# Another order of the first pair's copies, bits, maxima, scores and values, and of ScalarE's work in the last pairs, in a bucket-masked attention with a rational FFN

## The chip, the core and the metric

The kernel runs on one core of one Trainium2 chip. The metric is the device time of one execution in microseconds. Engines are named as the profile names them: PE (TensorE, with PEld for its weight loads), DVE (VectorE), ACT (ScalarE), POOL (GpSimd) and SP (SyncE, whose queue issues most DMAs).

## The reference

For 4 batches x 8 heads, 768 tokens and 64 channels, each query and key gets a 6-bit bucket from the signs of a projection. Scores between different buckets are masked; softmax and the product with V follow. The result is laid out as 3072 tokens x 512 channels and goes through an FFN whose nonlinearity is a rational function.

```python
q_bits = (np.einsum('bhsd,dk->bhsk', q, proj) > 0)      # likewise k_bits
mask = q_bucket[:, :, :, None] == k_bucket[:, :, None, :]
scores = np.where(mask, scale * q @ k.T, -1e9)
scores = scores - scores.max(-1)
attn = np.exp(scores); attn = attn / (attn.sum(-1) + 1e-9)
out = attn @ v
h = x @ w_in                                             # 512 -> 2048
g = (a0 + a1*h + a2*h**2 + a3*h**3) / (1 + |b0|*|h| + |b1|*h**2 + 1e-6)
y = g @ w_out                                            # 2048 -> 512
```

## The kernel before

**Pairs and steps.** The 32 heads are taken in 16 pairs (two heads of one batch). A pair has twelve steps: step s covers half `s // 6` of the queries (384 columns) and key tile `s % 6` (128 keys). `scores(p, s)` computes, for both heads, two accumulating matmuls of 128x384 into a PSUM bank of tag "s" (three banks, name `pss`), and ACT takes the exponential into one of seven E tiles; POOL adds E tiles into sums. `values(p, s)` multiplies V with the E tile of a step into the single bank of tag "v" (name `psv`); `values_out` copies the finished half out on ACT (a 1-column copy `col`, then `xo`). Each `scores` step is four matmul instructions in the profile, each `values` step four as well (plain float32, issued as two passes), and a `maxstep` two.

**Maxima ahead of the scores.** Before a pair's scores, its row maxima are found: `maxstep(p, j)` is one pass over all 768 keys for 128 queries of one head (bank pair of tag "psa", two of them, name `psm`) and a DVE reduction of 128x768. `shift_turn`, or `first_shift` for pair 0, turns the maxima into a row of the query operand (name `pst`), so that the score matmul subtracts them. The mask is done by extra rows of the operands as well: `bits`, `first_bits` and `second_bits` project queries and keys (name `psb`), DVE compares with zero, `penalties` scales on ACT, and `maskrows` moves the rows by DMA.

**Copies.** Queries and keys are split into a rounded part (`high`, an ACT cast of 128x768) and a remainder (`low`). For pair 0 the second head's operands are placed by extra ACT copies of 64x768, `first_cross`, in place of DMAs. `first_penalties` writes mask rows of pair 0's queries.

**The order is written out by hand.** Every piece of work is put in the dictionary `plan` by `at(p, s, function, ...)` at place 12 p + s; the places are decimals from the tables `MID` (pairs 1 to 14), `FIRST` (pair 0) and `LAST` (the last pairs). The plan is walked in order of place, and each engine, and SP's DMA queue, executes its instructions in just that order: an instruction that waits holds all that stands behind it on its engine. `warm(n)` issues n matmuls on a tile of zeros whose result nothing reads. `weights(i)` brings the FFN weights (stored as float64) in between: a DMA `wr`, ACT conversions `ws` and `wr`, DVE steps and a final ACT cast.

**FFN.** From the last pair on, `Ffn.step` runs GEMM 1 (`psh`), the rational terms, and GEMM 2 (`pso`) in blocks of 512 tokens.

Nearly all instructions are recorded by one helper line, 94 in the kernel before and 96 in the changed one; so they are told apart here by tile names.

Of the kernel before, what the change touches and what calls it, by code (L numbers as in the profile page):

```python
# [7 lines left out]
F32 = mybir.dt.float32  # L8
# [5 lines left out]
ALU = mybir.AluOpType  # L14
# [4 lines left out]
P = 128  # L19
S = 768  # L20
HQ = 384
NT = S // P
# [3 lines left out]
NPAIR = B * NHP  # L26
# [5 lines left out]
NFC = DFF // P  # L32
# [17 lines left out]
FIRST = dict(  # L50
    maxima1=[-0.04, -0.02, 5.52, 5.97, 6.42, 6.87, 7.32, 7.77, 8.22, 8.67, 9.12, 9.57], maxima2=9.5, rate2=0.82, high=[3.25, 3.53],
    low=[6.0, 7.3], bits=7.15, penalties=7.25, high_move=4.53, maskrows=8.2, second_low=-26.5, second_high=4.35, load_v=4.78, group=2,
    values=[-1.07, 2.65, 2.32, 2.35, 0.35, 0.61], values_out=3.02, high1=[-3.0, -3.2], low1=[-2.8, -2.95],
    high_move1=-2.7, load2=-2.6, load3=3.8, load4=9.0, penalties1=-24.26, maskrows1=-24.2,
    weights=[[-27.25, 6.64, 6.7, 11.42, 12.19, 18.75, 23.03], [8.03, 9.04, 9.24, 11.12, 14.81, 15.27, 15.99, 17.91, 46.81]],
    warm0=9, warm1=1, warm=3, warms=[3, 3, 3, 1, 1, 1], maxima00=[-4.3, -2.3, -4.2, -0.9, -1.2, -0.8], shift00=[-1.0, -0.2],
    shift0=[-0.08, -0.06], ahead=3, scores=[[-0.5, -0.4, -0.1], [0.1, 0.3, 0.4]], pen01=[-2.9, -0.35],
    second_high0=[-3.42, -3.4, -3.3, -3.25], load_v0=-3.3, bits1=-0.3, comp1=[-0.28, -0.27],
    maxima0=[-24.05, -23.8, -23.5, -0.9, -0.7, -0.1], turn1=[8.46, 13.26], rows1=[9.59, 14.35], turn2=8.61, third=6.9,
    third_weights=[1.44, 5.1, 5.5, 8.5, 9.5, 11.02, 11.035], steps={3: -1.0, 4: -0.8, 5: -0.6, 6: 5.4, 7: 6.5},  # L60
)
# [112 lines left out]
def attention(ctx, tc, nc, raw, ps_b, tail, tokens, early, operands_to_terms, ffn, load, QF, KF, v, w_in, w_out, wo_d, ident, cst, ones, prj,  # L174
# [147 lines left out]
    def first_cross(t):  # L322
        F, T = ((QF, Q1), (KF, K1))[t]
        nc.scalar.copy(T[0][0:64, 1 - t, :], F[0][64:128])
# [16 lines left out]
                                scalar1=-CLAMP, scalar2=-1.0, op0=ALU.max, op1=ALU.mult)  # L341


    def second_bits():
        for hf in range(2):
            ps = AV[1, hf] = ps_b.tile([P, 512], F32, tag="vs"[hf], bufs=(1, 3)[hf], name=f"psb1_{hf}")
            for t, F in enumerate((QF[1], KF[1])):
                o = 64 + 32 * t
                nc.tensor.matmul(ps[o : o + 32, 0:HQ], prj[:, t, :], F[:, hf * HQ : hf * HQ + HQ], start=True, stop=True)

    def second_compare(hf):
        nc.vector.tensor_scalar(out=MB[1][0][64:128, hf, :], in0=AV.pop((1, hf))[64:128, 0:HQ], scalar1=0.0,
                                scalar2=cst[64:128, 0:1], op0=ALU.is_gt, op1=ALU.subtract)

    def scores(p, s, heads=(0, 1)):
        hf, kt = divmod(s, NT)
# [119 lines left out]
    def at(p, s, f, *args):  # L476
        plan.setdefault(12 * p + s, []).append((f, args))
# [4 lines left out]

    for p in range(NPAIR):
        mid = 0 < p < NPAIR - 1
        n = MID["group"] if mid else (FIRST if p == 0 else LAST)["group"]
        for s in range(12):
            if p > 0 or s >= FIRST["ahead"]:
                at(p, FIRST["steps"].get(s, s) if p == 0 else s, scores, p, s)

            if p > 1:  # L490
                at(p - 2, FIRST["maxima2"] + FIRST["rate2"] * s if p == 2 else FIRST["third"] if p == 3 and s == 0 else MID["maxima"][s], maxstep, p, s)
            if s % n == n - 1:
                for i in range(s - n + 1, s + 1):
                    at(p, s + (MID["values"][s // n] if mid else (FIRST if p == 0 else LAST)["values"][s // n]), values, p, i)
            if s % NT == NT - 1:
                at(p, s + (LAST["vout14"] if (p, s) == (NPAIR - 2, 11) else MID["values_out"][s // n] if mid else (FIRST if p == 0 else LAST)["values_out"]), values_out, p, s // NT)
        for hf in range(2):
            at(p, 6 * hf + 9, values_store, p, hf)
        if p < NPAIR - 1:
            at(p, MID["sums"] if p < NPAIR - 2 else LAST["sums14"], sums, p)  # L500
            at(p, MID["sums_store"] if p < NPAIR - 2 else LAST["sumst14"], sums_store, p)
        if p > 1:
            for t in range(2):
                at(p - 2, (MID if p > 2 else FIRST)["high"][t], high, p, t)
                at(p - 2, MID["low"][t + t * p % 2] if p > 2 else FIRST["low"][t], low, p, t, nc.vector if p > 2 else nc.gpsimd)
# [12 lines left out]
        if p > 3:
            at(p - 4, MID["load"] if p > 4 else FIRST["load4"], load, p)
        if p % NHP == NHP - 1 and p + 1 < NPAIR:  # L520
            spread(p, MID["recips"], recips(p // NHP))
    for i in range(2 * NFC):
        o = 12 * (i // 2)
        w = list(FIRST["weights"][i]) if i < 2 else list(MID["weights"][i % 2])
        if i == 2:
            w = list(FIRST["third_weights"])
        if i == 2 * NFC - 4:
            w[0] = LAST["weights14"]
        if i == 2 * NFC - 1:
            w = w[:-4] + [w[-5] + x for x in MID["weights_last"]]  # L530
        spread(0, [o + x for x in w], weights(i))
# [29 lines left out]
    for h in range(2):  # L561
        for i in range(3):
            at(-2, FIRST["maxima00"][3 * h + i], maxstep, 0, NT * h + i)
            at(-2, FIRST["maxima00"][3 * h + i] + 0.01, warm, FIRST["warms"][3 * h + i])
# [268 lines left out]
```

## Time and profile before

| | us |
|---|---|
| median of three timed runs | 928.65 |
| the three runs | 1526.64, 928.65, 927.13 |
| profiled execution, device time | 924.78 |
| its span | 923.0 |
| PE busy | 914.9 (99%) |
| DVE busy | 839.9 (91%) |
| ACT busy | 653.7 (71%) |
| POOL busy | 425.7 (46%) |

The span is the time from the first to the last record of the profiled execution; 1.78 us lie around it. PE works without a visible break from about 8.4 us to the end, so that what counts of any other engine is the time for which PE has to wait for it. Busy shares over the whole span say little on the two stretches that the change touches: the first 50 us (pair 0 and the run into pair 1) and the stretch from 361 to 395 us (pairs 14 and 15, before the FFN). The granted clock of TensorE reads 1.00 in every stretch.

### The profile page before, as it was taken

To read this page: it belongs to the slowest core of one execution; us is meant where nothing else is said; L and a number is where in the kernel's file an instruction comes from. 1 tells how busy PE (TensorE), PEld (TensorE's weight loads), DVE (VectorE), ACT (ScalarE), POOL (GpSimd) and SP (SyncE) were. 2 spreads that over 40 slices of the span, in tenths; PEclk is the share of its full clock that TensorE was granted. 3 is DMA by queue.
4 is the path that set the end of the run, shared out by engine and by line. 5 is a ranking of instruction groups with operands and counts; after the bars stand their busy time and mean duration, and the time that the engine had idled before them with its cause. 6 is when DMAs were issued, how large, how long until landed. Compare 5 with 4: busy or idle time off the path is not lost.

```text
span 923.0 us, 13657 instructions
## 1 busy us (share of the span) xinstructions
PE 914.9 (99%) x4673; PEld 699.3 (76%) x4673; DVE 839.9 (91%) x1021; ACT 653.7 (71%) x1227; POOL 425.7 (46%) x363
## 2 busy tenths in 40 slices
PE   8999999999999999999999999999999999999998
PEld 5567767676767676678888888888888888888886
DVE  6799989988989899688998999999999989998996
ACT  7467777777777777886777677767676777667664
POOL 6577777677777777612322222222223222322221
PEclk9999999999999999999999999999999999999999
DMA  7678878787878778444402100400040013001001
GB/s 238 178 206 224 239 204 249 212 234 216 239 207 238 199 211 240 151 191 165 141 1 95 43 1 1 137 1 0 1 137 1 1 39 99 1 1 46 1 0 46
DMA packets 51097, 111.57 MB, mean 121 GB/s; under 512 B 9330, under 2 KB 19942, under 8 KB 51028
## 3 DMA queue, kind: packets, MB, share of 16 engines
q1 hardware_dynamic: 50596, 110.34, 40.4%
q8 instruction: 37, 0.61, 0.3%
q10 hardware_dynamic: 432, 0.36, 0.1%
q14 instruction: 32, 0.26, 0.1%
HBM read 56.82 MB, written 21.17 MB: 84 GB/s over the span
## 4 chain that ended last, share of the span: by engine, by line
PE 97%; DVE 1%; ACT 0%; DMA 0%; issue 0%; POOL 0%; POOLq 0%; ACTq 0%
PE psh L94 28%; PE pso L94 28%; PE pss L94 15%; PE psv L94 14%; PE psm L94 7%; PE psu L94 2%; PE psb L94 1%; DVE m L94 1%; DMA qkf<-qT 0%; PE pst L94 0%; PE pst_None L94 0%; POOL lo L94 0%; DVE ws L94 0%; ACT q L94 0%; ACT E L94 0%
## 5 line engine op out<-in xcount | busy, mean ns | idle before, releaser
L94 POOL TENSOR_TENSOR gl<-c,gh 128x512 fp32r<-128x512 f32 x95 | 135.8, 1429 | 384.7 <-ACT gh L94 374.6
L94 PE MATMUL pso<-wo,gh 128*128 128x512 f32 x768 | 235.9, 389 | 0.0
L94 DVE TENSOR_REDUCE m<-psm 128x1 f32<-128x768 f32 x192 | 180.6, 953 | 28.6 <-PE psm L94 21.0
L94 ACT ACTIVATE E<-pss 128x384 f32<-128x384 f32 x384 | 166.8, 492 | 40.2 <-PE pss L94 32.3
L94 POOL TENSOR_TENSOR acc<-E,E 128x384 f32<-128x384 f32 x124 | 146.2, 1198 | 95.7 <-ACT E L94 95.7
L94 PE MATMUL pss<-q,k 128*128 128x384 f32 (+2 forms) x768 | 171.2, 346 | 0.9 <-ACT E L94 0.7
L94 PEld LDWEIGHTS pso<-wo,gh 128*128 128x128 f32 x768 | 144.2, 188 | 29.9
L94 ACT ACTIVATE h<-psh 128x512 f32<-128x512 f32 x96 | 57.4, 598 | 132.9 <-PE psh L94 132.8
L94 PEld LDWEIGHTS pss<-q,k 128*128 128x128 f32 (+2 forms) x768 | 134.5, 190 | 22.1 <-issue 8.0
L94 PE MATMUL psh<-xh,wi_hi 128*128 128x512 f32 x384 | 149.6, 390 | 0.0
L94 PE MATMUL psh<-xl,wi_hi 128*128 128x512 f32 x384 | 149.4, 389 | 0.0
L94 PE MATMUL psh<-xh,wi_lo 128*128 128x512 f32 x384 | 149.4, 389 | 0.0
L94 PE MATMUL pso<-wo,gl 128*128 128x512 f32 x384 | 148.9, 389 | 0.0
L94 DVE SCALAR_TENSOR_TENSOR c<-c,ab,r 128x512 f32<-128x512 f32 x96 | 138.7, 1445 | 0.0
L94 POOL TENSOR_TENSOR acc<-acc,E 128x384 f32<-128x384 f32 x123 | 132.5, 1096 | 3.4 <-ACT E L94 3.0
L94 PE MATMUL psv<-E,v 128*64 128x385 f32 x768 | 131.9, 492 | 0.0
L94 PE MATMUL psm<-k,q 76*128 76x384 f32 (+1 forms) x384 | 100.6, 344 | 1.8 <-ACT k L94 1.5
L94 PEld LDWEIGHTS psv<-E,v 128*64 128x64 f32 x768 | 52.0, 137 | 65.5 <-issue 63.6
L94 DVE SCALAR_TENSOR_TENSOR w<-h,absb,w 128x512 f32<-128x512 f32 x96 | 72.9, 759 | 15.2 <-ACT w L94 15.0
L94 PEld LDWEIGHTS psh<-xh,wi_hi 128*128 128x128 f32 x384 | 72.0, 188 | 16.0 <-issue 1.2
L94 PEld LDWEIGHTS psh<-xh,wi_lo 128*128 128x128 f32 x384 | 72.1, 188 | 15.0
L94 PEld LDWEIGHTS pso<-wo,gl 128*128 128x128 f32 x384 | 72.0, 188 | 15.0
(77 smaller groups left out, 1213.1 us busy)
## 6 DMA issues: line engine op xcount, KB each, us to landing
q<-q SPq DMA_DIRECT2D x45, 192.0 KB
k<-k SPq DMA_DIRECT2D x45, 192.0 KB
wr<-w_in SPq DMA_DIRECT2D x16, 512.0 KB
wr<-w_out SPq DMA_DIRECT2D x16, 512.0 KB
wo_d<-wr SPq DMA_DIRECT2D x16, 512.0 KB
wo<-wo_d SPq DMA_DIRECT2D x16, 512.0 KB
qkf<-qT SPq DMA_DIRECT2D x16, 384.0 KB
qkf<-kT SPq DMA_DIRECT2D x16, 384.0 KB
```

What stands on the lines that cost most here:

```text
L94: return self.tc.keep_in_program_order(issue(*args, **kwargs))
```

## The change

Four things are edited, most of them by numbers in the tables.

- `first_cross(1)`, the copy of k for the first head, is issued ahead of `high(0, 1)` in place of behind the comparisons.
- `second_bits`, the projection for pair 1's bits, is split in its two halves, both in one bank of tag "v", and the halves go between the first maxima of pair 0. Eight of the twelve warm matmuls that stood between maxima go.
- In pairs 0 and 1 the maxima, scores and values take new places: the values of pair 0 are issued one step at a time, in place of in groups of two and more, between single maxima and scores. The bits and mask rows of pair 2, the shift rows of pair 1, and the loads of V for pair 1 and of one `w_out` block take new places with them.
- In pairs 14 and 15 some ACT work takes new places: `values_out` of pair 14's first half and of pair 15, and the conversions of three weight blocks.

```diff
 FIRST = dict(
...
-    values=[-1.07, 2.65, 2.32, 2.35, 0.35, 0.61], values_out=3.02, high1=[-3.0, -3.2], low1=[-2.8, -2.95],
+    values=[-0.4, -0.07, -0.03, 5.0, 5.2, 5.3, 6.3, 7.4, 8.2, 9.1, 9.6, 10.4], values_out=[5.31, 10.42], high1=[-3.0, -3.2],
...
 LAST = dict(
-    group=6, values=[0.28, 0.44], values_out=1.39, vout14=3.03,
+    group=6, values=[0.28, 0.44], values_out=0.46, vout14=[3.5, 3.03],
+    hi14=17.05, weights15=[5.1, 5.11],
...
-    def second_bits():
-        for hf in range(2):
-            ps = AV[1, hf] = ps_b.tile([P, 512], F32, tag="vs"[hf], bufs=(1, 3)[hf], name=f"psb1_{hf}")
-            for t, F in enumerate((QF[1], KF[1])):
-                o = 64 + 32 * t
-                nc.tensor.matmul(ps[o : o + 32, 0:HQ], prj[:, t, :], F[:, hf * HQ : hf * HQ + HQ], start=True, stop=True)
+    def second_bits(hf):
+        if hf == 0:
+            MS[2] = ps_b.tile([P, 512], F32, tag="v", name="psb1")
+        for t, F in enumerate((QF[1], KF[1])):
+            o = 64 * hf + 32 * t
+            nc.tensor.matmul(MS[2][o : o + 32, 0:HQ], prj[:, t, :], F[:, hf * HQ : hf * HQ + HQ], start=True, stop=True)
...
-            if s % n == n - 1:
+            if p == 0:
+                at(p, FIRST["values"][s], values, p, s)
+            elif s % n == n - 1:
...
     warm(FIRST["warm1"])
+    first_cross(1)
     high(0, 1)
...
     first_compare(0, 1)
-    first_cross(1)
     low(0, 1, nc.gpsimd)
...
-    at(-2, FIRST["bits1"], second_bits)
     for hf in range(2):
+        at(-2, FIRST["bits1"][hf], second_bits, hf)
         at(-2, FIRST["comp1"][hf], second_compare, hf)
```

**PE, the first maxima of pair 0.** The names are `psm0_j` for the maximum step j of pair 0, `psw` for a warm matmul, `pst0_0_0` for the turn of the first three maxima, `psb1` for pair 1's bits and `pss0_s_h` for a score step of head h. Before:

```order
L94 MATMUL psm0_1_260<-k1_0_177,q1_0_179 128x384 x2
L94 LDWEIGHTS E6_153
L94 MATMUL psw5_264<-E6_153 128x384
L94 LDWEIGHTS E6_153
L94 MATMUL psw5_264<-E6_153 128x384
L94 LDWEIGHTS E6_153
L94 MATMUL psw5_264<-E6_153 128x384
L94 MATMUL psm0_7_268<-k1_0_177,q1_0_179 128x384 x2
L94 LDWEIGHTS E6_153
L94 MATMUL psw6_272<-E6_153 128x384
L94 MATMUL pst0_0_0_274<-cst_75,m0_214 1x128 x3
L94 MATMUL psm0_6_279<-k1_0_177,q1_0_179 128x384 x2
```

After, from the second maximum on:

```order
L96 MATMUL psm0_2_223<-k1_0_177,q1_0_179 128x384 x2
L96 MATMUL psb1_227<-qkf1_77,prj_73 32x384 x2
L96 MATMUL psm0_1_259<-k1_0_177,q1_0_179 128x384 x2
L96 MATMUL psb1_227<-qkf1_77,prj_73 32x384 x2
L96 MATMUL psm0_7_265<-k1_0_177,q1_0_179 128x384 x2
L96 LDWEIGHTS E6_153
L96 MATMUL psw4_269<-E6_153 128x384
L96 MATMUL pst0_0_0_271<-cst_75,m0_214 1x128 x3
L96 MATMUL psm0_6_276<-k1_0_177,q1_0_179 128x384 x2
L96 MATMUL pss0_0_0_280<-q1_0_179,k1_0_177 128x384
L96 MATMUL pss0_0_0_280<-q2_0_202,k2_0_203 128x384
L96 MATMUL psm0_8_284<-k1_0_177,q1_0_179 128x384 x2
```

In place of the warm matmuls stand the two halves of pair 1's bits, two matmuls each, and the first scores now stand between `psm0_6` and `psm0_8`. In the kernel before the four bits matmuls stood in one piece behind `pss0_1_0`.

**ACT, from the end of pair 0's scores to the start of pair 1's.** The names are the E tiles, `ws1` and `wr1` for the conversion of a `w_out` block, `col0_1` and `xo0_1` for pair 0's second half of values, `q1_3` for the cast of pair 3's queries. Before:

```order
L94 ACTIVATE ws1_516<-wr1_515 128x512
L94 ACTIVATE wr1_515<-wr1_515 128x512
L94 ACTIVATE E3_150<-pss0_10_0_579 128x384
L94 ACTIVATE E3_150<-pss0_10_1_583 128x384
L94 ACTIVATE E4_151<-pss0_11_0_594 128x384
L94 ACTIVATE E4_151<-pss0_11_1_598 128x384
L94 CAST q1_3_604<-qkf3_420 128x768
L94 ACTIVATE E5_152<-pss1_0_0_620 128x384
L94 ACTIVATE E5_152<-pss1_0_1_624 128x384
L94 ACTIVATE E6_153<-pss1_1_0_634 128x384
L94 ACTIVATE E6_153<-pss1_1_1_638 128x384
L94 CAST k1_3_647<-qkf3_420 128x768
```

After:

```order
L96 ACTIVATE E3_150<-pss0_10_0_533 128x384
L96 ACTIVATE E3_150<-pss0_10_1_537 128x384
L96 ACTIVATE E4_151<-pss0_11_0_557 128x384
L96 ACTIVATE E4_151<-pss0_11_1_561 128x384
L96 COPY col0_1_598<-psv0_1_493 128x1
L96 ACTIVATE xo0_1_599<-psv0_1_493,col0_1_598 128x384
L96 ACTIVATE ws1_545<-wr1_544 128x512
L96 ACTIVATE wr1_544<-wr1_544 128x512
L96 CAST q1_3_605<-qkf3_421 128x768
L96 ACTIVATE E5_152<-pss1_0_0_617 128x384
L96 ACTIVATE E5_152<-pss1_0_1_621 128x384
L96 ACTIVATE E6_153<-pss1_1_0_631 128x384
```

Behind the last exponential of pair 0 now stand five pieces of ACT work in a row, the first of which waits for the last values of pair 0, ahead of the first exponential of pair 1. Before, one stood there (the cast); the conversion stood two score steps earlier and the copy out behind pair 1's third step.

**ACT, in pair 15.** The names are as above, `sr14` for the sums of pair 14 and `xh0_3` for the cast of FFN tokens. Before:

```order
L94 CAST wr29_4406<-ws29_4407 128x512
L94 COPY sr14_4515<-psu14_4506 128x384
L94 ACTIVATE E1_148<-pss15_3_0_4518 128x384
L94 ACTIVATE E1_148<-pss15_3_1_4522 128x384
L94 ACTIVATE E2_149<-pss15_4_4526 128x384 x2
L94 ACTIVATE E3_150<-pss15_5_4538 128x384 x2
L94 ACTIVATE ws30_4490<-wr30_4489 128x512
L94 CAST xh0_3_4484<-y0_2_4536 128x512
L94 ACTIVATE wr30_4489<-wr30_4489 128x512
L94 ACTIVATE E4_151<-pss15_6_0_4567 128x384
L94 ACTIVATE E4_151<-pss15_6_1_4571 128x384
L94 COPY col15_0_4576<-psv15_0_4548 128x1
```

After:

```order
L96 COPY sr14_4501<-psu14_4492 128x384
L96 ACTIVATE E1_148<-pss15_3_0_4504 128x384
L96 ACTIVATE E1_148<-pss15_3_1_4508 128x384
L96 ACTIVATE E2_149<-pss15_4_4512 128x384 x2
L96 ACTIVATE E3_150<-pss15_5_4524 128x384 x2
L96 CAST wr29_4389<-ws29_4390 128x512
L96 ACTIVATE ws30_4477<-wr30_4476 128x512
L96 ACTIVATE wr30_4476<-wr30_4476 128x512
L96 CAST xh0_3_4471<-y0_2_4522 128x512
L96 COPY col15_0_4551<-psv15_0_4537 128x1
L96 ACTIVATE xo15_0_4552<-psv15_0_4537,col15_0_4551 128x384
L96 ACTIVATE E4_151<-pss15_6_0_4558 128x384
```

The cast of `wr29` goes from ahead of `sr14` and six exponentials to behind them, `wr30` from behind `xh0_3` to ahead of it, and `col15_0` and `xo15_0` from behind the two exponentials of `pss15_6` to ahead of them.

More of the change, by code (lines that the diff above doesn't have):

```diff
@@ L50 @@
 FIRST = dict(
-    maxima1=[-0.04, -0.02, 5.52, 5.97, 6.42, 6.87, 7.32, 7.77, 8.22, 8.67, 9.12, 9.57], maxima2=9.5, rate2=0.82, high=[3.25, 3.53],
-    low=[6.0, 7.3], bits=7.15, penalties=7.25, high_move=4.53, maskrows=8.2, second_low=-26.5, second_high=4.35, load_v=4.78, group=2,
-    values=[-1.07, 2.65, 2.32, 2.35, 0.35, 0.61], values_out=3.02, high1=[-3.0, -3.2], low1=[-2.8, -2.95],
-    high_move1=-2.7, load2=-2.6, load3=3.8, load4=9.0, penalties1=-24.26, maskrows1=-24.2,
-    weights=[[-27.25, 6.64, 6.7, 11.42, 12.19, 18.75, 23.03], [8.03, 9.04, 9.24, 11.12, 14.81, 15.27, 15.99, 17.91, 46.81]],
@@ L56 @@
[L56 to L60, printed above, removed]
+    maxima1=[-0.04, -0.01, 5.05, 5.15, 5.25, 5.35, 6.2, 6.4, 7.3, 7.5, 8.1, 8.3], maxima2=9.5, rate2=0.82, high=[3.25, 3.53],
@@ new lines @@
+    low=[3.6, 3.65], bits=6.15, penalties=6.25, high_move=4.53, maskrows=6.5, second_low=-26.5, second_high=4.35, load_v=6.6,
+    values=[-0.4, -0.07, -0.03, 5.0, 5.2, 5.3, 6.3, 7.4, 8.2, 9.1, 9.6, 10.4], values_out=[5.31, 10.42], high1=[-3.0, -3.2],
+    low1=[-2.8, -2.95], high_move1=-2.7, load2=-2.6, load3=3.8, load4=9.0, penalties1=-23.55, maskrows1=-23.5,
+    weights=[[-27.25, 6.64, 6.7, 11.42, 12.19, 18.75, 23.03], [8.03, 10.5, 10.55, 11.12, 14.81, 15.27, 15.99, 17.91, 46.81]],
+    warm0=9, warm1=1, warm=3, warms=[3, 0, 0, 0, 1, 0], maxima00=[-4.3, -2.3, -4.2, -0.9, -1.2, -0.55], shift00=[-1.0, -0.2],
@@ L61 @@
+    shift0=[-0.08, -0.06], ahead=3, scores=[[-0.6, -0.4, -0.3], [0.1, 0.3, 0.4]], pen01=[-2.9, -0.28],
+    second_high0=[-3.42, -3.4, -3.3, -3.25], load_v0=-3.3, bits1=[-4.1, -2.2], comp1=[-0.18, -0.17],
+    maxima0=[-24.25, -24.15, -0.9, -0.7, -0.5, -0.1], turn1=[6.35, 9.05], rows1=[6.36, 9.06], turn2=8.61, third=6.9,
+    third_weights=[1.44, 5.1, 5.5, 8.5, 9.5, 11.02, 11.035],
+    steps={3: -1.0, 4: -0.8, 5: -0.6, 6: -0.02, 7: 5.1, 8: 6.1, 9: 7.2, 10: 8.0, 11: 9.0},
 )
 LAST = dict(
-    group=6, values=[0.28, 0.44], values_out=1.39, vout14=3.03,
+    group=6, values=[0.28, 0.44], values_out=0.46, vout14=[3.5, 3.03],
@@ L341, in first_shift @@
                                 scalar1=-CLAMP, scalar2=-1.0, op0=ALU.max, op1=ALU.mult)
-    def second_bits():
-        for hf in range(2):
-            ps = AV[1, hf] = ps_b.tile([P, 512], F32, tag="vs"[hf], bufs=(1, 3)[hf], name=f"psb1_{hf}")
-            for t, F in enumerate((QF[1], KF[1])):
-                o = 64 + 32 * t
-                nc.tensor.matmul(ps[o : o + 32, 0:HQ], prj[:, t, :], F[:, hf * HQ : hf * HQ + HQ], start=True, stop=True)
+    def second_bits(hf):
[4 more added lines that the diff above has]
+            nc.tensor.matmul(MS[2][o : o + 32, 0:HQ], prj[:, t, :], F[:, hf * HQ : hf * HQ + HQ], start=True, stop=True)
     def second_compare(hf):
-        nc.vector.tensor_scalar(out=MB[1][0][64:128, hf, :], in0=AV.pop((1, hf))[64:128, 0:HQ], scalar1=0.0,
-                                scalar2=cst[64:128, 0:1], op0=ALU.is_gt, op1=ALU.subtract)
+        sl = slice(64 * hf, 64 * hf + 64)
+        nc.vector.tensor_scalar(out=MB[1][0][64:128, hf, :], in0=MS[2][sl, 0:HQ], scalar1=0.0,
+                                scalar2=cst[sl, 0:1], op0=ALU.is_gt, op1=ALU.subtract)
     def scores(p, s, heads=(0, 1)):
@@ L484, in attention @@
         mid = 0 < p < NPAIR - 1
-        n = MID["group"] if mid else (FIRST if p == 0 else LAST)["group"]
+        n = MID["group"] if mid else LAST["group"]
         for s in range(12):
@@ L491, in attention @@
                 at(p - 2, FIRST["maxima2"] + FIRST["rate2"] * s if p == 2 else FIRST["third"] if p == 3 and s == 0 else MID["maxima"][s], maxstep, p, s)
-            if s % n == n - 1:
+            if p == 0:
+                at(p, FIRST["values"][s], values, p, s)
+            elif s % n == n - 1:
                 for i in range(s - n + 1, s + 1):
-                    at(p, s + (MID["values"][s // n] if mid else (FIRST if p == 0 else LAST)["values"][s // n]), values, p, i)
+                    at(p, s + (MID if mid else LAST)["values"][s // n], values, p, i)
             if s % NT == NT - 1:
-                at(p, s + (LAST["vout14"] if (p, s) == (NPAIR - 2, 11) else MID["values_out"][s // n] if mid else (FIRST if p == 0 else LAST)["values_out"]), values_out, p, s // NT)
+                at(p, FIRST["values_out"][s // NT] if p == 0 else
+                   s + (LAST["vout14"][s // NT] if p == NPAIR - 2 else MID["values_out"][s // n] if mid else LAST["values_out"]), values_out, p, s // NT)
         for hf in range(2):
@@ L528, in attention @@
             w[0] = LAST["weights14"]
+        if i == 2 * NFC - 3:
+            w[5] = LAST["hi14"]
+        if i == 2 * NFC - 2:
+            w[1:3] = LAST["weights15"]
         if i == 2 * NFC - 1:
@@ L563, in attention @@
             at(-2, FIRST["maxima00"][3 * h + i], maxstep, 0, NT * h + i)
-            at(-2, FIRST["maxima00"][3 * h + i] + 0.01, warm, FIRST["warms"][3 * h + i])
+            if FIRST["warms"][3 * h + i]:
+                at(-2, FIRST["maxima00"][3 * h + i] + 0.01, warm, FIRST["warms"][3 * h + i])
             at(0, FIRST["maxima0"][3 * h + i], maxstep, 0, NT * h + 3 + i)
```

## The prediction

> **What bounds the kernel now.** First the page, for the engine that sets the end; then the busy time by stretch, for the places where that engine has slack; then the chain of waits there.
>
> ```profile
> span 923.0 us, 13657 instructions
> PE 914.9 (99%) x4673; PEld 699.3 (76%) x4673; DVE 839.9 (91%) x1021; ACT 653.7 (71%) x1227; POOL 425.7 (46%) x363
> ```
>
> The busy time in the stretches of interest (columns: stretch, length, then busy time and instructions of PE, PEld, DVE, ACT, POOL, granted clock, DMA share, GB/s):
>
> ```profile
> 25.80:49.43 23.63, 23.14 (x127) 14.60 (x127) 19.16 (x25) 11.39 (x24) 12.09 (x11) 1.00 0.62 179
> ...
> 100.00:361.00 261.00, 261.00 (x1615) 183.81 (x1615) 235.45 (x271) 191.69 (x418) 198.76 (x180) 1.00 0.79 223
> ```
>
> From 100 to 361 us PE has no gap at all, and the clock is 1.00. So whatever PE is spared before 100 us, or between 361 and 395 us, moves all that follows forward by as much, and whatever it waits longer there is paid in full. The change touches just these two stretches. The chain of waits (start, length, what) at the start:
>
> ```profile
> 6.90 0.61 ACT q L94
> ...
> 7.52 0.84 ACT k L94
> ...
> 8.40 0.64 PE psm L94 x2
> ...
> 9.06 3.57 DVE m L94 x4
> ...
> 14.84 1.42 PE psb L94 x8
> ...
> 25.13 0.76 PE pst L94 x6
> ...
> 27.15 0.70 PE pss L94 x4
> 27.85 0.35 PE psm L94 x2
> 28.20 1.45 PE psv L94 x8
> 29.64 0.57 PE psm L94 x2
> ...
> 31.11 0.96 DVE m L94
> ...
> 32.11 1.50 PE psb L94 x16
> ...
> 35.63 1.83 DVE m L94 x2
> ```
>
> Until 9 us the path runs over ACT's copies, then over four DVE reductions in a row (3.57 / 4 = 0.89 each), and from then on over PE, with DVE on the path at a few places. PE's prices are here too: a score step 0.70, a maximum 0.35, the same 0.57 behind values.
>
> **The change, part by part.** *The copy of k first.* What the first maximum waits for, by ACT's and DVE's own records:
>
> ```profile
> 5.22 0.84 ACT L94 CAST k<-qkf 128x768 fp32r<-128x768 f32 x1 [0.31 <-DMA qkf<-kT]
> 6.90 0.61 ACT L94 ACTIVATE q<-mb,hs 32x384 fp32r<-32x384 f32 x1 [0.84 <-POOL lo L94]
> ```
>
> ```profile
> 6.32 1.27 DVE L94 TENSOR_SCALAR k<-psb_first,cst 32x384 fp32r<-32x384 f32 x2 [0.23 <-PE psb_first L94]
> 7.62 0.61 DVE L94 TENSOR_SCALAR mb<-psb_first,cst 32x384 fp32r<-32x384 f32 x1
> ```
>
> ACT idles 0.84 before 6.90, for POOL's remainder. The 64-row copy (0.84 in the chain) now runs at 5.22, the whole cast of k behind it fills that gap to 6.9, and the mask rows still end at 7.51. The first maximum then waits for DVE's comparisons, which end at 7.59: it starts near 7.65, not 8.40. DVE is free at 8.23, so the first reduction starts at 8.31, not 9.06. **-0.75.** The cast of k ends about 0.85 later, under POOL's first remainder, which ends at 6.86: no cost.
>
> *Pair 1's bits between the maxima, eight warm matmuls less.* The bits (1.42) leave the dense stretch behind 14.84: -1.42. They cost something where they go. Each half takes 0.71 of PE, and entering and leaving plain float32 costs more: by the rows
>
> ```profile
> 28.13 1.51 PE L94 MATMUL psv<-E,v 128*64 128x385 f32 x8
> ...
> 56.04 4.10 PE L94 MATMUL psv<-E,v 128*64 128x385 f32 x24
> ```
>
> one instruction is (4.10 - 1.51) / 16 = 0.162, so the group's 1.45 in the chain holds 1.45 - 8 x 0.162 = 0.15 beside its work, and the maximum behind takes 0.57 for 0.35: together 0.37 per group. A maximum with half the bits is then 0.35 + 0.71 + 0.37 = 1.43 on PE against 0.89 for a reduction on DVE, twice, with two bank pairs to soften it. Followed through: the first three warm matmuls stay, of about 0.16 as the instruction above, so that the maxima start at 7.65, 8.48, 9.67 and 10.87, and each reduction can start 0.66 behind its maximum (8.40 to 9.06); the fourth runs from 11.55 to 12.50, where it ended at 12.63. Of the 0.75 only 0.13 is left there: **-1.42 + 0.62 = -0.80.**
>
> The warm matmuls cost nothing before, since DVE's reductions set the pace, and save nothing now.
>
> *ACT's pass over the bits.* The penalties of pair 1 (0.93) stood ahead of the third exponential and now stand behind six; the rows:
>
> ```profile
> 16.96 0.93 ACT L94 ACTIVATE mb<-mb,cst 64x768 fp32r<-64x768 f32 x1 [0.92 <-DVE mb L94]
> ...
> 19.01 0.87 ACT L94 ACTIVATE E<-pss 128x384 f32<-128x384 f32 x2 [0.21 <-PE pss L94]
> ```
>
> PE may run three score banks ahead of ACT. From `pss0_0_1` on ACT needs 0.55 until the first exponential (a head of scores of 0.35 and the 0.21 of idling in the row above), three of 0.44, the pass, and one more: 3.24 until the bank for `pss0_4_1` is free, a little less as starts overlap. PE gets there in six heads of 0.35 and a maximum of 0.35, 2.45. **+0.7**; nothing if the first exponentials start early, 0.93 at most.
>
> *Values one step at a time.* One group more before the turn that ends at 25.89: **+0.35**. From there to pair 1's third step (25.80 to 49.43) the work is the same: 18 maxima (6.3), 8 score steps (5.6), 40 value instructions (6.5) and the bits of pair 2 (1.50), 19.9 in all. Before there are 6 float32 groups (2.2), which leaves 23.63 - 22.1 = 1.5 of waits; these are the DVE pieces at 31.11 and 35.63, where two maxima follow each other faster than DVE reduces them. Afterwards a score or value step stands between nearly all maxima, so that these waits go, but there are 11 groups: 19.9 + 4.1 = 24.0. **+0.3**, from -1.5 (waits gone, groups free) to +1.85 (waits kept).
>
> *The queue of ACT before pair 1.* Rows of the pieces that now stand together ahead of pair 1's first exponential:
>
> ```profile
> 39.33 0.68 ACT L94 ACTIVATE ws<-wr 128x512 f32<-128x512 f32 x1
> 39.89 0.71 ACT L94 ACTIVATE wr<-wr 128x512 int32<-128x512 uint32 x1
> ...
> 45.29 0.83 ACT L94 CAST q<-qkf 128x768 fp32r<-128x768 f32 x1
> ...
> 51.18 0.17 ACT L94 COPY col<-psv 128x1 f32<-128x1 f32 x1
> 51.38 0.58 ACT L94 ACTIVATE xo<-psv,col 128x384 f32<-128x384 f32 x1
> ```
>
> The column copy waits for pair 0's last values. From their end ACT needs 0.1 + 0.2 + 0.5 + 0.56 + 0.6 + 0.75 + 0.44 = 3.15, by starts, until the first exponential frees a bank; PE needs it after maxima of 0.57, 0.35 and 0.35 and three heads of scores (1.05), at 2.3. Nothing else hides it: **+0.85**, and 0 if the last values come late for another reason.
>
> *Pairs 14 and 15.* The chain and ACT's records there:
>
> ```profile
> 385.67 2.69 PE pss L94 x14
> ...
> 388.51 0.87 ACT E L94 x2
> ...
> 389.43 1.74 PE pss L94 x8
> ```
>
> ```profile
> 380.90 0.62 ACT L94 CAST wr<-ws 128x512 fp32r<-128x512 f32 x1 [1.30 <-DVE ws L94]
> ...
> 385.99 0.62 ACT L94 CAST xh<-y 128x512 fp32r<-128x512 f32 x1 [1.22 <-DVE y L94]
> ...
> 387.10 0.86 ACT L94 ACTIVATE E<-pss 128x384 f32<-128x384 f32 x2
> ```
>
> PE waits here from 388.36 to 389.43 for the exponentials of `pss15_7`, which stand behind 1.30 and 1.22 of ACT waiting for DVE. The first of these waits is passed by work that is ready (`sr14` and six exponentials, some 1.3 earlier), the second is filled with `wr30`, and the copy out (0.75) goes ahead of the exponentials while `pss15_6` is still being computed. Two exponentials (0.87) earlier than 388.51 are enough: **-0.9**, from -0.3 (the token cast still waits for DVE until 385.96) to -1.2 (with what pair 14's copy out cost). The FFN then starts as much earlier.
>
> **Sum:** -0.75 - 0.80 + 0.7 + 0.35 + 0.3 + 0.85 - 0.9 = -0.25. The profiled execution took 924.78 (1.78 beside its span), which makes 924.5. The two timed runs that agree are 2.35 and 3.87 above it (927.13, and 928.65, the median), so I predict **927.0**, 2.5 above the sum.
>
> **The rivals.** *ACT never binds* (30%): both bank waits, 0.7 and 0.85, vanish, since PE comes late to them anyhow. For it: in the stretch to 49.43 ACT is busy for 11.39 of 23.63. Against: the queues are short ones, and a share doesn't show them. 924.5 - 1.55 = 923.0; timed 925.5.
>
> *The weight block comes late* (20%), and the change is slower. V of pair 1 and the `w_out` block are now issued by SP behind the shift rows and the four mask-row moves of pair 2. ACT's conversion of this block stands ahead of pair 1's first exponential and would hold it, and so PE, which stops at the fourth bank. SP's issues, and how long such a block can take, by one in the middle:
>
> ```profile
> 38.32 0.78 SPq L94 DMA_DIRECT2D k<-mb  x1
> ...
> 40.73 1.42 SPq L94 DMA_DIRECT2D q<-mt  x2
> ...
> 181.96 0.39 SPq L94 DMA_DIRECT2D wr<-w_out  x1
> ```
>
> ```profile
> 188.90 0.68 ACT L94 ACTIVATE ws<-wr 128x512 f32<-128x512 f32 x1 [0.93 <-DMA wr<-w_out]
> ```
>
> 6.9 from issue to use. Behind the bits of pair 2 PE has, by the prices above, 11.0 of work to pair 0's last values (8 maxima, 3 score steps, 24 value instructions, 6 groups). DVE's comparison and ACT's pass take some 2.0 of it, SP's six issues 1.42 + 4 x 0.78 = 4.5, and V's some 0.6: I estimate the block's issue some 4 before ACT wants it. So it decides at 4 us of landing; at 6.9 PE waits 2.9 more: 927.4, timed 929.9. The Trainium skill ("DMA: Bandwidth & Descriptors", section "Anatomy of one DMA — SWDGE (gpsimd) path") gives about 2.0 us fixed plus the bytes at 436 GB/s, for another issuing path. For 512 KB that is an estimate of 3.2 us, by which this rival would not happen; the row of 6.9 us, under load, is twice that.
>
> *The clock falls* (4%). With eight warm matmuls less PE idles a little between maxima. From the second maximum to the first scores of the second head PE has 7 maxima, the bits, two turns of 0.76 and three heads of scores, some 7.1 with the groups; at half clock twice that, in place of 8.2 that pass anyhow: +6, 930.5, timed 933. Against: before, PE stood idle ahead of 8.40 for longer than any gap that is left, and the clock stayed 1.00. The Trainium skill ("TensorE: Matmul & The Clock Gate", section "A second HAM failure mode: psum-queue depth-cycling") tells of kernels whose PE idles briefly while cycling through PSUM banks and whose clock falls again and again; by this rule the removal is harmful. The trace of before, paced by the same two bank pairs, doesn't show it, though with the warm matmuls in place.
>
> *The gain doesn't arrive* (6%): the FFN's first loads set its start, and what is won before is lost there: between 924.5 and 926, timed up to 928.5.
>
> **Numbers.** My forecast holds 40%, with 926 to 928.5 as its own range in timed runs. With the first rival below it and most of the second above, and the run-to-run spread of 1.5, 8 in 10 lie between 922.3 and 930.5. A measurement can tell about 2% here, 18.5 us. No case comes near that: faster 1%, within 97%, slower 2%, the ends for what I haven't thought of.
>
> **What would show it.** The first reduction at 8.3; the fourth ending near 12.5; a PE wait for ACT's exponentials near 19 us (0.7) and one at pair 1's second step (0.9); value groups of four with 0.3 lost around each; no DVE wait between maxima from 26 to 40 us; no PE wait at pair 15. If the ACT conversion ahead of pair 1 is released by the DMA of `w_out`, the slow rival holds; if the clock column leaves 1.00 below 20 us, the clock. I am wrong altogether if the dense stretch isn't moved by what the first 50 us and pair 15 give.

## The result, and the profile after

The changed kernel takes 936.21 us (median of six runs, 931.56 to 937.37) against 927.23 for the kernel before, measured beside it: a ratio of 1.0079 with a 95% interval of 1.0057 to 1.0100 (the quotient of the two medians, 1.0097, lies inside it). It is slower, though within 2%, and it lies 9.2 above the forecast of 927.0, outside the range that ended at 930.5. The profiled execution takes 931.56 where the one of before took 924.78: 6.78 to be found. The profiled execution is the fastest of the six, with a mean granted clock of 0.996 where the other five read 0.991 to 0.995, so more time may go to a lower clock in those than this trace shows.

First the page and the busy time by stretch, as for the kernel before, with one more stretch (columns: stretch, length, busy time and instructions of PE, PEld, DVE, ACT, POOL, granted clock, DMA share, GB/s):

```profile
span 929.7 us, 13648 instructions
...
PE 919.2 (99%) x4665; PEld 699.8 (75%) x4665; DVE 841.6 (91%) x1021; ACT 653.7 (70%) x1227; POOL 424.6 (46%) x363
```

```profile
25.80:49.43 23.63, 23.19 (x124) 12.63 (x121) 15.51 (x19) 10.22 (x21) 11.13 (x10) 1.00 0.54 150
50.00:60.00 10.00, 6.93 (x30) 4.94 (x30) 8.56 (x11) 5.49 (x11) 4.62 (x4) 0.66 0.78 194
100.00:361.00 261.00, 261.00 (x1609) 183.06 (x1609) 236.23 (x271) 191.74 (x417) 198.97 (x181) 1.00 0.78 224
```

From 100 to 361 us nothing has changed: PE has no gap. The loss is ahead of it, and the row from 50 to 60 us stands out twice: PE works for 6.93 of 10 us, and at a mean clock of 0.66. The chain of waits shows how it gets there (start, length, what):

```profile
7.54 0.85 PE psm L96 x2
...
11.93 0.97 DVE m L96
...
17.30 0.60 PE pss L96 x2
...
19.21 0.93 ACT mb L96
...
20.71 0.62 PE pss L96 x2
...
25.63 0.75 PE pst L96 x6
26.38 0.55 PE psm L96 x2
...
43.49 0.52 SPq L96
...
44.06 6.22 DMA wr<-w_out
...
50.30 0.67 ACT ws L96
...
50.99 0.44 DVE wr L96
...
52.15 0.88 DVE m L96
...
53.07 1.01 PE psm L96 x2
54.08 1.28 PE pss L96 x4
55.36 0.64 PE psm L96 x2
56.00 1.28 PE pss L96 x4
57.28 0.64 PE psm L96 x2
57.92 2.36 PE psu L96 x16
60.28 0.90 PE pss L96 x4
...
63.92 2.08 PE psv L96 x11
```

The view ends at 66 us and cuts the last row off; these values take 4.03 in all, as before. SP issues the `w_out` block at 44.06, it lands 6.22 later, ACT converts its first part, DVE has a piece of the conversion to do, and only then comes the reduction for which PE waits. That wait is 3.63 long, by PE's own record, and DVE's record says what DVE waited for:

```profile
53.07 1.01 PE L96 MATMUL psm<-k,q 76*128 76x384 f32 x2 [3.63 <-DVE m L96]
```

```profile
50.99 0.43 DVE L96 TENSOR_SCALAR wr<-wr 128x512 int32<-128x512 int32 x1 [2.95 <-ACT ws L96]
```

Behind the pause a score step takes 1.28 where it took 0.70, a maximum 0.64 for 0.35, the sums (`psu`) 2.36 for 1.50. In stretches of one us:

```profile
49.00:50.00 1.00, 0.44 (x3) 0.12 (x1) 0.00 (x0) 0.00 (x0) 0.00 (x0) 1.00 0.94 361
...
52.00:53.00 1.00, 0.00 (x0) 0.00 (x0) 1.00 (x3) 1.00 (x3) 0.00 (x0) 0.98 1.04 216
53.00:54.00 1.00, 0.93 (x3) 0.93 (x4) 1.00 (x3) 0.02 (x1) 0.00 (x0) 0.50 0.73 146
...
59.00:60.00 1.00, 1.00 (x12) 0.20 (x4) 0.59 (x1) 0.00 (x0) 1.00 (x2) 0.61 0.99 207
```

The clock drops to a half at 52.96 (0.98 of a stretch is 0.04 at half) and comes back at 59.78 (0.61 is 0.78 at half): 6.82 us. What it costs follows from the six groups of the chain, each against its price at full clock: 0.39 + 0.58 + 0.29 + 0.58 + 0.29 + 0.86 = 3.0 (the first maximum against the 0.62 that one takes after any wait).

Where the 6.78 go, by the starts of the same work in both kernels. One row of the kernel before is needed, pair 1's first values:

```profile
56.11 4.03 PE psv L94 x24
```

The first pair's last turn ends at 26.38 for 25.89: +0.49. From there to pair 1's first values it is 37.54 (63.92 - 26.38) for 30.22 (56.11 - 25.89): +7.32, of which 3.63 are the pause, 3.0 the half clock, and 0.7 the rest. The FFN's first matmul starts at 401.8 for 395.1, so 1.1 of the 7.8 by which pair 1's first values are late (63.92 for 56.11) come back in the last pairs:

```profile
L96 PE MATMUL psh<-xh,wi_hi x21: 389/389/504, 401.8 to 420.0; 128*128 128x512 f32 x21
```

```profile
L94 PE MATMUL psh<-xh,wi_hi x26: 389/389/504, 395.1 to 419.4; 128*128 128x512 f32 x26
```

### The profile page after: what moved, and what is told of

It is laid out like the page before. It is cut to its first block, busy times and chain, and to the rows that moved or that the text cites. A ratio compares the mean times of both kernels' runs of the same rounds, so it can differ in the third digit from the quotient of the medians.

```text
span 929.7 us, 13648 instructions
## 1 busy us (share of the span) xinstructions
PE 919.2 (99%) x4665; PEld 699.8 (75%) x4665; DVE 841.6 (91%) x1021; ACT 653.7 (70%) x1227; POOL 424.6 (46%) x363
## 4 chain that ended last, share of the span: by engine, by line
PE 96%; DMA 1%; DVE 1%; ACT 1%; SPq 1%; issue 0%; POOL 0%; DVEq 0%; POOLq 0%
PE psh L96 28%; PE pso L96 28%; PE pss L96 15%; PE psv L96 14%; PE psm L96 7%; PE psu L96 3%; PE psb L96 1%; DMA wr<-w_out 1%; SPq L96 1%; DVE m L96 0%; DMA qkf<-qT 0%; PE pst_None L96 0%; DVE ws L96 0%; POOL lo L96 0%; ACT E L96 0%
## 5 line engine op out<-in xcount | busy, mean ns | idle before, releaser
L96 DVE SCALAR_TENSOR_TENSOR c<-c,ab,r 128x512 f32<-128x512 f32 x96 | 135.6, 1412 | 0.0
L96 PEld LDWEIGHTS psh<-xl,wi_hi 128*128 128x128 f32 x384 | 72.1, 188 | 15.1
```

What stands on the lines that cost most here:

```text
L96: return self.tc.keep_in_program_order(issue(*args, **kwargs))
```

## The experiments

The runs were made in three groups and one last run, each with its own runs of the kernel before (median 928.51, 924.83 and 924.91 for the groups, 928.60 for the last run). Ratios are to those.

**The block earlier.** In the changed kernel, the DMA of the `w_out` block alone goes ahead of pair 1's shift rows.

```diff
-    weights=[[...], [8.03, 10.5, 10.55, 11.12, ...]],
+    weights=[[...], [6.2, 10.5, 10.55, 11.12, ...]],
```

> The changed kernel with one number different: the DMA of the first w_out block is issued ahead of pair 1's shift rows and pair 2's mask rows (place 6.2 in place of 8.03), so SP issues it about 12 us earlier. Theory A (the late block held ACT and DVE, hence PE, and the pause took the clock down): the 3.6 us PE wait near 50 us and the stretch at half clock vanish, 6 to 9 us less than the changed kernel, 926 to 928 timed, no row of ACT released by that DMA. Theory B (the new order of maxima and values, with 5 more float32 groups and fewer warm matmuls, is what costs): at most 1.6 us less (ACT's own 1.61 wait), 934 or more.

Ratio 1.0053 (1.0039 to 1.0067): 2.4 us less than the changed kernel, between what the two theories said, and with both intervals it could be next to nothing or 5. The block is issued at 31.16 and is no longer waited for. But PE pauses all the same, for 1.9. The chain:

```profile
46.85 0.85 PE psv L96 x4
...
47.72 0.17 ACT col L96
...
47.91 0.58 ACT xo L96
48.49 0.56 ACT ws L96
...
49.08 0.44 DVE wr L96
...
51.15 0.63 PE psm L96 x2
```

So there are two conditions, not one. DVE's piece waits for ACT's, and ACT's stands behind the column and token copies, which wait for pair 0's last values. The late block only makes the wait longer. The clock falls here too, by stretches of one us from 51.92 to 58.74: 6.82 us again. It falls a second time in this execution, at 249.90, far from the edit (see the last section).

**The conversion later.** In the changed kernel, the block's conversion moves behind more of pair 1, and the load stays where it is.

```diff
-    weights=[[...], [8.03, 10.5, 10.55, 11.12, 14.81, ...]],
+    weights=[[...], [8.03, 13.2, 13.25, 14.6, 14.81, ...]],
```

> The changed kernel with the block still loaded late, but its conversion on ACT and DVE moved behind pair 1's first scores (places 13.2, 13.25, 14.6 in place of 10.5, 10.55, 11.12). Theory A: the DMA still lands as late (6 us after its issue), but nothing that PE needs stands behind it: no PE wait of 3.6, clock 1.00, 926 to 929. Theory B: no change from 936.

Ratio 1.0085 (1.006 to 1.011), no gain. The wait for the block is gone, and another took its place; DVE's record:

```profile
55.62 1.01 DVE L96 TENSOR_TENSOR lo<-qkf,q 128x768 fp32r<-128x768 f32 x1 [3.05 <-DMA q<-lo]
```

The instruction writes the tile that a transfer for pair 2, at 48.44 in the chain, still reads; that one takes 7.05. With V and the block behind the mask rows, SP's other transfers start later as well and run together: 15 GB/s from 36 to 44 us, 388 from 47 to 51. PE waits 2.3 and 1.5, and the clock is at a half from 60.32 to 67.14.

**The pause filled.** In the changed kernel, 22 matmuls whose result nothing reads are put where PE pauses.

```diff
+    def fill(n):
+        ps = ps_b.tile([P, 512], F32, tag="s", bufs=3, name="psfill")
+        for _ in range(n):
+            nc.tensor.matmul(ps[:, 0:HQ], K1[1][0:77, 0, 0:P], Q1[1][0:77, 0, 0:HQ], start=True, stop=True)
...
+    at(0, 12.5, fill, 22)
```

> The changed kernel with 22 useless matmuls (22 x 0.163 = 3.6 us, result never read) issued on PE just where it pauses near 50 us; they add work and take no wait away. Theory A with the clock as a consequence of the pause: PE's wait is filled, the granted clock stays 1.00 up to 62 us, and the 3.9 us that the half clock cost in the profiled execution go; 3 to 6 us less than the changed kernel, 930 to 933. If the clock falls for another reason (few warm matmuls at the start, float32 groups), it still falls and the time stays at 935 to 938 or rises by up to 3.6.

Ratio 1.0038 (1.0016 to 1.0060), 0.41% or 3.8 us less than the changed kernel (each against its own runs of before; 1 to 7 us with both intervals). The mean clock reads 1.000 in six of the ten timed runs, where none of the changed kernel's read more than 0.996. The profile: the 22 matmuls take 3.84 in the chain, and the clock stays.

```profile
50.00:60.00 10.00, 9.73 (x63) 8.15 (x62) 9.83 (x13) 6.89 (x16) 5.01 (x5) 1.00 0.86 207
```

The next maximum starts at 53.18, for 53.07 without the filling: the pause is as long as it was, only filled. So about half of the loss is the half clock, and the clock falls because PE pauses. The two profiled executions lie only 0.64 apart (930.92 and 931.56), since this one has a pause of 1.73 before 247.53 that the other has not (see the last section).

**The last pairs alone, twice.** The kernel before with the edits of pairs 14 and 15, and nothing else.

```diff
-    group=6, values=[0.28, 0.44], values_out=1.39, vout14=3.03,
+    group=6, values=[0.28, 0.44], values_out=0.46, vout14=[3.5, 3.03],
+    hi14=17.05, weights15=[5.1, 5.11],
```

> The kernel before with the last pairs' edit alone (ACT's work in pairs 14 and 15 at the new places; the first pair as before). By my prediction's term -0.9; by the two traces, where the FFN's first matmul comes 6.67 later after a delay of 7.81, -1.1: so 1 us less than before, about 0.999, and no PE wait for exponentials in pair 15.

> The kernel before with the part of the change in pairs 14 and 15 alone, timed a second time, since the first interval reached 0.9999. Theory: 1.1 us less, as the traces of both show between pair 14 and the FFN: ratio 0.998 to 0.9993. Rival (the first result was spread): 0.9995 or more.

Ratios 0.9983 (0.9967 to 0.9999) and 0.9982 (0.9970 to 0.9993). Before and in the second of these runs, the stretch of the last pairs:

```profile
361.00:395.00 34.00, 33.23 (x194) 20.47 (x192) 26.56 (x31) 26.25 (x61) 22.75 (x20) 1.00 0.53 164
```

```profile
361.00:395.00 34.00, 34.00 (x207) 22.00 (x197) 28.06 (x33) 27.71 (x64) 25.07 (x22) 1.00 0.56 172
```

PE's gap of 0.77 is gone. This is the part of the change that gains, and this kernel is faster than both (by 0.2% than the kernel before).

**The loads back in the gap.** In the changed kernel, the loads of V and of the block go back to where SP idles, and ACT's part of the conversion goes ahead of the column and token copies.

```diff
-    low=[3.6, 3.65], ..., load_v=6.6,
+    low=[3.6, 3.65], ..., load_v=4.78,
...
-    weights=[[...], [8.03, 10.5, 10.55, 11.12, ...]],
+    weights=[[...], [4.8, 9.04, 9.24, 11.12, ...]],
```

> The changed kernel, with the loads of V and of the w_out block put back into the gap in which SyncE idles (ahead of pair 1's shift rows), and ScalarE's part of the block's conversion put ahead of pair 0's last column and token copies. Theory (what costs is that two transfers left the gap, and that VectorE's in-order queue then holds the maxima): both are issued before 35 us, no wait of PE for a reduction above 1 us between 44 and 56 us, clock 1.00 in 50-60 us, pair 1's third step within 1 us of the kernel before (49.4), time 0 to 2 us below the kernel before (ratio 0.998 to 1.000). Rival (the new order of maxima, scores and values is itself slower there): PE still pauses for over 1.5 us before 56 us, ratio 1.003 or more.

Ratio 1.0024 (1.0014 to 1.0034). The loads are issued at 31.81 and 32.44, the pause is gone (what is left are three waits of PE of 0.1 each between 49.9 and 53 us), and the clock holds:

```profile
50.00:60.00 10.00, 9.73 (x58) 6.54 (x60) 9.84 (x12) 7.13 (x17) 7.71 (x6) 1.00 0.89 215
```

So these places cost 5.1 us of the 7.3 (1.0079 - 1.0024 = 0.55%; 3 to 7 us with both intervals). But I expected this version to be below the kernel before, and pair 1's third step within 1 us of it; it starts 2.5 later (51.93 for 49.43). The rest of the change costs more than my sum gave it.

**The loads late, in the kernel before.** The same from the other side: nothing but the places of these two loads.

```diff
-    low=[6.0, 7.3], ..., load_v=4.78, group=2,
+    low=[6.0, 7.3], ..., load_v=8.3, group=2,
...
-    weights=[[...], [8.03, 9.04, 9.24, 11.12, ...]],
+    weights=[[...], [8.35, 9.04, 9.24, 11.12, ...]],
```

> The kernel before, with only the loads of V and of the w_out block moved behind the four mask-row moves of pair 2, as the change has them. Theory (the late loads alone do it): the block is issued near 39 us instead of 29.8 and lands near 45, ScalarE and VectorE wait for it with exponentials and maxima behind, PE pauses 2 to 5 us and its clock falls: ratio 1.004 to 1.010. Rival (the loads' place is harmless, the change's order of the work is at fault): ratio below 1.001.

Ratio 1.0073 (1.0061 to 1.0085): two moved DMAs make the kernel before nearly as slow as the whole change. The chain is the same, with the block landing in 4.66 here, and so is the wait of DVE:

```profile
39.67 4.66 DMA wr<-w_out
...
44.35 0.67 ACT ws L94
...
46.39 1.01 PE psm L94 x2
47.40 1.28 PE pss L94 x4
```

```profile
45.04 0.43 DVE L94 TENSOR_SCALAR wr<-wr 128x512 int32<-128x512 int32 x1 [4.84 <-ACT ws L94]
```

```profile
45.00:46.00 1.00, 0.00 (x0) 0.00 (x0) 0.96 (x2) 1.00 (x4) 0.00 (x0) 0.55 0.80 316
...
51.00:52.00 1.00, 1.00 (x5) 0.00 (x1) 0.22 (x1) 0.00 (x0) 0.00 (x0) 0.54 1.06 280
```

Half clock from 45.10 to 51.92, 6.82 once more.

**The copy of k alone.** The kernel before with `first_cross(1)` moved as in the change.

> The kernel before with one part of the change alone: the copy of k for the first pair's scores ahead of the cast of k. As predicted: first reduction at 8.3 instead of 9.06, the start 0.75 us shorter, span 922.3, ratio 0.9992. Rival (the copy is delayed or something later takes it back): first reduction within 0.2 of 9.06, or the span unchanged.

Ratio 1.0009 (1.0001 to 1.0018), no gain. Seven of the eleven timed runs lie at 924.55 to 925.46, where all but one of before lie (924.67 to 925.60), and four at 927.31 to 927.46. The profiled execution is one of these four and has, at 241 us, the pause of 1.73 of the last section, which is far from the edit. In this execution the first reduction starts at 9.43, later than before. ACT has the copy done in time (its two k copies end at 6.83); the maximum waits for DVE's comparisons, and these for PE's first bits:

```profile
4.37 1.50 PE L94 MATMUL psb_first<-qkf,prj 128*32 128x384 f32 x4
```

```profile
7.49 1.27 DVE L94 TENSOR_SCALAR k<-psb_first,cst 32x384 fp32r<-32x384 f32 x2 [0.98 <-PE psb_first L94]
```

In the kernel before, with the same instructions ahead of them, the first of these groups took 0.86 and the comparisons started at 6.32. Over the thirteen profiled executions the first group takes from 0.84 to 1.50. Where k's copy stands at its old place, the first reduction starts at 8.94 to 9.06 for groups of 0.84 to 1.19, since ACT is later than all of them, and at 9.34 for one of 1.49. Where the copy is first, it is 8.29 to 8.44 for groups of 0.84, 8.58 and 8.75 for 1.25 and 1.21, and 8.80 to 9.43 for 1.49 and 1.50. So at the first reduction most of the 0.75 is there when PE's first matmuls are quick. That it reaches the end is not shown: the fastest of the eleven runs is 924.55, the fastest of before 924.67, and no trace shows this kernel with a quick first group, so that the rival (something later takes it back) stays open.

**ACT's pass earlier.** The version with the loads in the gap, and DVE's comparisons and ACT's pass for pair 1's bits as early as they stood before.

```diff
-    ... penalties1=-23.55, maskrows1=-23.5,
+    ... penalties1=-24.26, maskrows1=-24.2,
...
-    ... comp1=[-0.18, -0.17],
+    ... comp1=[-0.28, -0.27],
```

> As the run with the loads in the gap, and ScalarE's pass over pair 1's bits put ahead of the second head's first exponentials. As predicted for that term: the PE wait for exponentials near 19-20 us goes, 0.5 to 0.7 us less than with the loads in the gap alone. Rival (the pass costs the same wherever it stands): within 0.2 us of it.

Ratio 1.0025 (1.0015 to 1.0036), the same as without it (1.0024). The wait for exponentials near 19 us is gone, and DVE's comparisons, now ahead of a maximum (1.2 in the chain from 15.54), hold PE instead, for 1.46 by its record. The last turn ends at 26.80, for 26.58 without the edit. Without it PE then waits 0.25 for pair 1's mask rows of k, so that the next maximum starts at 26.80 with the edit and at 26.83 without.

**The start alone, and all but the start.** The kernel before with the part ahead of 25 us as in the change; and the version with the loads in the gap, with that part as before. The diff is that of the first, with places cut out.

```diff
+    first_cross(1)
     high(0, 1)
...
-    warm=3, warms=[3, 3, 3, 1, 1, 1], maxima00=[..., -0.8], ...
+    warm=3, warms=[3, 0, 0, 0, 1, 0], maxima00=[..., -0.55], ...
...
-    ... bits1=-0.3, comp1=[-0.28, -0.27], ... penalties1=-24.26, ...
+    ... bits1=[-4.1, -2.2], comp1=[-0.18, -0.17], ... penalties1=-23.55, ...
```

> The kernel before with the part of the change ahead of 25 us alone: copy of k first, pair 1's bits between the first maxima, eight warm matmuls less, pair 1's penalties behind six exponentials; values, maxima, scores, loads and the last pairs as before. As predicted (-0.75 - 0.80 + 0.7): the last turn ends near 25.0 instead of 25.89, time 0.85 below the kernel before (ratio 0.9991). Rival, from the rows of the changed kernel (last turn at 26.38 with one value group more, 0.35): the start doesn't gain but loses 0.1 to 0.2, last turn at 26.0 to 26.1, ratio 1.000 to 1.0005.

> The run with the loads in the gap, with the part ahead of 25 us as in the kernel before: what is left of the change is the order of maxima, scores and single value steps, the conversion's places, and the last pairs. Theory (this order costs 1.6 to 1.7 between the last turn and pair 1's values, and the last pairs give 1.1 back): from the end of the last turn to pair 1's first values 31.8 us, against 30.22 before; time 0.5 above the kernel before, ratio 1.000 to 1.001. Rival (the loss comes from the start's state, late loads and exponentials carried along): 30.3 to 30.8, and time 0.5 to 1 below the kernel before.

The start alone: 1.0013 (1.0004 to 1.0022), 1.2 us more where I had forecast 0.85 less. Its last turn ends at 27.60, worse than both expectations; it is one of the executions with a slow first group (1.49), and PE waits 0.54 for exponentials and 0.45 for a reduction right ahead of the turns. All eleven runs (925.58 to 926.98) lie above the median of before, 924.91. All but the start: 1.0014 (1.0005 to 1.0023), and from the last turn to pair 1's values 31.76, as the theory said, against 30.22; the time is 0.8 more than it said:

```profile
25.39 0.75 PE pst L96 x6
...
57.90 4.03 PE psv L96 x24
```

Put together, by the timed runs: the start costs 1.2, the order from 26 to 56 us with the last pairs 1.3, which makes 2.5 where the version with the loads in the gap measured 2.2; the places of the two loads and of the conversion make up the other 5.1. That the parts simply add is not shown. By the traces the start costs 1.71 alone, but 0.69 in the version with the loads in the gap (26.58 for 25.89) and 0.49 in the changed kernel; the order costs 1.54 in the one run and 1.85 in the other (58.65 - 26.58 = 32.07 for 30.22); the last pairs give 1.1 back. And in the four kernels that have the new order and issue the block ahead of pair 1's shift rows, some 2.2 us lie outside the span, for 1.78 in the kernel before; why is not shown.

## Why the prediction was wrong

**The rival that came true, and its price.** The step that failed most is that the sum puts the late weight block, and what it holds, at nothing: the choice between the forecast and that rival, and within the rival the words "ACT's conversion ... would hold it, and so PE, which stops at the fourth bank", with 2.9 for PE. The runs showed a pause of 3.63 in its place, and 3.0 of half clock behind it. The rival's times were good: the block was issued 4.6 before ACT wanted it (44.06 to 48.69, where ACT begins its wait of 1.61), where I estimated 4, and it landed in 6.22, between the 4 at which it decides and the row of 6.9. But I gave 20% to the longer landing, though the row that I had quoted for such a block said 6.9. The Trainium skill's figure ("DMA: Bandwidth & Descriptors", section "Anatomy of one DMA — SWDGE (gpsimd) path"), which I worked out to an estimate of 3.2 for another issuing path, is half of the 6.22 measured, and the measurement decides. And the path was another: not the score banks, but DVE, whose piece of the conversion stands in order ahead of pair 2's maxima. I had followed the new places through ACT's and SP's queues and not through DVE's. So it is luck that 2.9 lies near 3.63: ACT's own wait for the block was only 1.61.

**The clock.** What no rival priced is what a pause does afterwards. I placed the fall of the clock ahead of 18 us, by the missing warm matmuls, where nothing fell; it came behind a pause of 3.6 at 49 us, and cost 3.0 by the records, 3.8 by the timed runs with the pause filled. With the pause of 3.6 as measured, and nothing else changed, the rival would have come to 924.5 + 3.6 + 3.0 = 931.1, within 0.5 of the profiled execution. That it comes so near is helped by errors that nearly cancel. Put on the 924.5 of my sum, they are: +1.0 for the start (+0.49 for -0.5), +3.6, +3.0, -0.45 for the rest from 26 us on (+0.7 for +1.15), -0.2 for the last pairs, which makes 931.5. And the 2.5 that I added for timed runs was too little: their median lies 4.65 above the profiled execution.

**Copy of k first, -0.75.** Right in its mechanism as far as the first reduction: the first maximum at 7.54 (7.65 forecast) and the first reduction at 8.58 (8.31) in the changed kernel. What I missed is that this puts the path on PE's first matmuls, which vary by 0.66 from run to run, and that the old place hides it for groups up to 1.19.

**Bits between the maxima, -0.80.** Wrong in both of its halves. From the first maximum (8.40 before, 7.54 after) to the fourth reduction's end it is 5.36 for 4.23, +1.13, where I had +0.62: the three warm matmuls and the first, slower maximum make the second one start 1.36 later, not 0.83. And of the 1.42 removed behind 14.84 only 0.80 came back: DVE's reductions, one of them now ahead of the second turn, hold PE to 16.56 there (DVE's records after).

```profile
13.60 2.96 DVE L96 TENSOR_REDUCE m<-psm 128x1 f32<-128x768 f32 x3
16.59 0.56 DVE L96 TENSOR_SCALAR q<-pst 1x384 fp32r<-1x384 f32 x1
```

The bits had lain beside DVE's work. So the second head's first scores start at 17.30, only 0.53 earlier than in the kernel before, and not 1.55:

```profile
17.83 0.43 PE pss L94 x2
```

**ACT's pass +0.7 and one group +0.35.** Right in sum: from those scores to the end of the last turn 9.08 for 8.06, +1.02 for 1.05. The PE wait for exponentials is there, 0.5 by PE's records. But moving the pass back gains nothing, so it was no cost of that place alone.

**From 25.80 on, +0.3.** Mis-sized. I took 1.5 of PE's 23.63 for waits that would go, as what was left over after adding up prices; the row beside it said 23.14 busy, so only 0.49 were there to go. With the loads in the gap, from the last turn's end (26.58) to the third step (51.93) it is 25.35 for 23.54 (25.89 to 49.43): +1.81, at the upper end that I gave (+1.85, groups paid and waits kept). The groups are as priced: 0.80 for four instructions, and 0.55 for the maximum behind.

**ACT's queue before pair 1, +0.85.** Right that the queue binds, wrong in path and size. In the run with the block early, where ACT waits for no DMA, the queue holds PE for 1.90, and through DVE's piece and the reduction behind it, not through exponentials. So of the 3.63 some 1.9 belong to this term, and the rest to the late block. The version with the loads in the gap doesn't test it, since its conversion stands elsewhere.

**Pairs 14 and 15, -0.9.** Right: 1.1 in the trace, 1.6 and 1.7 in timed runs (with intervals that hold 1.1), and no wait of PE for ACT is left there.

**The signs.** The one that I named for the slow rival, an ACT conversion released by the DMA of `w_out`, is what the trace shows; the sign for the clock was looked for in the wrong stretch.

## What to carry to other kernels

When a plan in which every queue is in order is edited, follow each moved piece through all the engines that share it: here two loads left a gap in which SP idled, and what stopped PE was a small step on DVE, two engines away. Price a pause of PE of some 2 us or more at its length plus, should the clock fall behind it, half of the 3.4 or 6.8 us for which it stayed low here, and look where an edit can make one; filling it with useless matmuls saved about half of the loss here. And before calling a wait something that can be won, compare it with the idle time that the stretch's own row leaves.

## What the runs showed of the hardware

- The clock was at a half for 6.82 us in four kernels, by the stretches of one us: after a pause of 3.63, of 2.88, of 1.90, and after two of 2.3 and 1.5 with 1.7 between. It fell in three more places, behind the pause of 1.73 to 1.75, between 240 and 253 us, that the last point below tells of, for 3.4 us each: with the block early and in the kernel before with late loads (both at 249.90), and with the last pairs alone (243.58). In five other executions with that pause it stayed at 1.00, the second one of the last pairs alone among them. So a pause of 1.7 can be enough, and need not be. The edits don't cause these falls: beside the first group, runs of the kernel before too read mean clocks of 1.000 (924.99 us), 0.998 (928.51) and 0.994 (931.80). The falls came 0.7 to 3.5 us after the last pause began, in four of the seven cases when PE was already working again. Two executions have two falls each, and these begin 197.98 and 204.80 apart. The Trainium skill ("TensorE: Matmul & The Clock Gate", section "Part 1: The HAM clock gate") tells of a free-running window of 4096 cycles, 3413 ns; one and two of these are 3.41 and 6.83, and 58 and 60 of them are 197.97 and 204.80, which the seven falls bear out. It asks for an idle window of about 3.4 us; here 1.73 was enough in three cases of eight, and the measurement decides. What sets these three apart is not shown; where the pause lies in the window would be a candidate.
- A 512 KB load issued by SP took 6.22 in the changed kernel and 4.66 in the kernel before with late loads; the transfers behind it, issued while it runs, differ between the two.
- PE's first four matmuls on data took 0.84 to 1.50 with nothing changed ahead of them, while the clock column read 1.00. The cause is not shown.
- In 8 of the 13 profiled executions PE waits 1.7 once between 200 and 361 us, for a reduction that stands on DVE behind `rz`, which waits for a small DMA. The kernel with the last pairs alone shows it in both of its profiles, the one with the loads in the gap in its one, the same kernel with ACT's pass earlier does not; the edits are all far from there. In the first profile of the last pairs alone the DMA `rs<-s_d` lands at 233.43 and `rz` runs until 236.82, 3.36 by DVE's record for 1.01 in the kernel before, with the reduction further behind it; why it takes longer is not shown.
